# Subtracting k's maxima on VectorE out of PSUM, token tables as narrow as the tokens seen, and three rows for every free place: a fused linear attention, top-2 mixture of experts and soft mixture of experts on one Trainium2 core

## The chip, the cores and the metric

The program runs on one core of one Trainium2 chip. The metric is the device time of one execution in microseconds. A core has five engines that run their own instruction streams in order and wait for one another by semaphores: TensorE (PE in the rows, with its weight loads as PEld), VectorE (DVE), ScalarE (ACT), GpSimd (POOL) and SyncE (SP, which here only issues DMAs). Matmul results land in PSUM, everything else that the engines read and write is in SBUF, and DMAs move data between SBUF and DRAM.

## The reference, cut to what matters

```python
# attention, per batch and head (8 batches, 8 heads, 576 positions, 64 wide)
q_s = softmax(q, over the 64)          # q - max, exp, / sum
k_s = softmax(k, over the 576)         # k - np.max(k, axis=2), exp, / sum
kv = einsum('bhsd,bhse->bhde', k_s, v)
x = einsum('bhsd,bhde->bhse', q_s, kv) # -> x: 4608 tokens x 512

# mixture of experts: 8 experts, 512 -> 1024 -> 512, two per token
noisy = x @ w_gate + log1p(exp(x @ w_noise)) * noise
top2 = argpartition(-noisy, 2)[:, :2]; top2_w = softmax(noisy[top2])
for e in range(E):
    for k in range(2):
        mask = top2[:, k] == e
        out[mask] += top2_w[mask, k, None] * (relu(x[mask] @ w1[e]) @ w2[e])

# soft mixture of experts over out: logits = out @ phi (32 slots), softmax over
# tokens and over slots, 8 small experts on the slots, then c @ slot_out
```

The maximum of k runs over the positions, which lie on the partitions of a k tile, so it can't be taken by one reduction along the free axis.

## The kernel before

**Stages.** Attention takes the batches in four pairs (`i` = 0 to 3), each pair in nine tiles of 128 tokens: four whole tiles for the first batch, four for the second, and a ninth tile whose lower 64 partitions belong to the first batch and whose upper 64 to the second. A step list, `FIRST`, fixes the order in which the attention's steps are written: `lk`, `lv`, `lq` load, `km`/`ks`/`ke` take k's maxima, subtract them and apply exp for one batch of the pair, `qm`/`qs`/`qe` do the same for a third of the pair's q, `kv` multiplies k and v, `qt` transposes a q tile, `ou` makes the outputs of one tile, `ga` starts the gate of some tiles and `bg` advances it by a piece, `ze` writes zeros, `pf` and `pl` plan the experts. The framework's scheduler then places each engine's instructions by its own timeline, so the order on an engine follows the list only roughly. A second list, `MIX`, holds the last of the attention; it is interleaved with the first ten expert blocks.

**k's maxima** (`k_max`, `k_sub`, lines 200 to 226). For each batch of a pair, VectorE takes the maximum of the four whole tiles into `km` (L203, L205), then of `km` and the half tile (L207, 64 partitions). TensorE transposes `km` into a PSUM tile `pt` (L210), VectorE reduces it to `mT` (L212), TensorE transposes `mT` back, broadcast to all partitions, into another `pt` (L219), ScalarE copies that to SBUF as `ms` (L221), and GpSimd subtracts `ms` from the half tile (L223) and from the four whole tiles in two instructions of 1024 (L226). One of the eight cases, `ks0.1v`, has its three subtractions on VectorE. All `pt` tiles of this stage (also those of `qt`, `kt` and `kw`) come from one pool of three PSUM banks.

**Token tables.** Every pair's tokens go through a gate in two parts, of six tiles and of three (`gate`, lines 329 to 451). It ranks each token among those of its expert, writes the place as a row and a column, makes one-hot matrices of the rows (`ob`, L422, L423) and of the columns (`oa`, L431, 288 columns: 36 for each of 8 experts) on VectorE, multiplies them on TensorE (L441) and adds the result into the table `tab` (L446, or L449 to L451). The first half of the tokens (pairs 0 and 1) is planned first (`plan_first`), and its experts' blocks begin while the attention of pairs 2 and 3 runs.

**Expert blocks.** A block gathers rows of `xtab` by an index column for each 128 tokens (L694, GpSimd), transposes them (L766), multiplies by `w1` (L781) and `w2` (L811) and adds the weighted result to `x2` by a scatter that accumulates (L816 on VectorE, L817 on GpSimd). There are ten blocks of two index columns from the first half, then as many blocks of three columns as the plan asks for (five here, in nested branches, L902), then blocks of two. Gathers and scatters stand in one queue on GpSimd, in which gathers for a later block come ahead of a block's own scatters. Places of a table that no token fills get row `NTOK + p` of `xtab` and `x2`, one for each partition, so that two free places in one partition hit the same row. Scatters of one block of two are declared free of each other; the three scatters of a block of three are not, since free places occur there.

**Tail.** The soft mixture of experts reads `x2` back and ends the program.

Of the kernel before, what the change touches and what calls it, by code (L numbers as in the profile page):

```python
# [21 lines left out]
P = 128  # L22
# [12 lines left out]
TE = 36  # L35
NSLOT = 32
GT = 6
NZ, CW = 4, 6
EPS = 1e-9

# [31 lines left out]
def gate_consts(k, ap):  # L72
    nc = k.nc

    ltf = ap.tile([P, P], F32, name="ltf")
    nc.gpsimd.affine_select(out=ltf, in_=k.ones, pattern=[[1, P]], compare_op=ALU.is_gt, fill=0.0, base=0, channel_multiplier=-1)
    k.lt = ap.tile([P, P], F16, name="lt")
    nc.vector.tensor_copy(k.lt, ltf)
    k.ones16 = ap.tile([P, P], F16, name="ones16")
    nc.vector.tensor_copy(k.ones16, k.ones)  # L80

    it = ap.tile([P, E * TE], I32, name="it")
    nc.gpsimd.iota(it, pattern=[[1, E * TE]], base=0, channel_multiplier=0)
# [11 lines left out]
    k.eoff = ap.tile([P, E], F32, name="eoff")  # L95
    nc.vector.tensor_scalar(k.eoff, k.ef, float(TE * P), None, op0=ALU.mult)
    pd = ap.tile([P, 1], I32, name="pd")
    nc.gpsimd.iota(pd, pattern=[[0, 1]], base=NTOK + 1, channel_multiplier=1)
    k.pad1 = ap.tile([P, 1], F32, name="pad1")
    nc.vector.tensor_copy(k.pad1, pd)  # L100

    k.tril = ap.tile([P, E, E], F32, name="tril")
    nc.gpsimd.affine_select(out=k.tril, in_=k.ones[:, :64].rearrange("p (e f) -> p e f", e=E), pattern=[[1, E], [-1, E]], compare_op=ALU.is_gt, fill=0.0, base=0, channel_multiplier=0)

    k.tri = ap.tile([P, E + 1, E], F32, name="tri")
    nc.gpsimd.affine_select(out=k.tri, in_=k.ones[:, :72].rearrange("p (r e) -> p r e", e=E), pattern=[[1, E + 1], [-1, E]], compare_op=ALU.is_gt, fill=0.0, base=0, channel_multiplier=0)
    k.e7 = ap.tile([P, E], F32, name="e7")
    nc.vector.tensor_scalar(k.e7, k.ef, float(E) - 2.5, None, op0=ALU.subtract)


def attention(k):
# [3 lines left out]
    with ExitStack() as ctx:  # L115
# [27 lines left out]
        after = [None]  # L143
        cnt = ac.tile([P, E], F16, name="cnt")
        lgrs, rqas, seen = {}, {}, []
        tab = k.tab = ac.tile([P, E * TE], F32, name="tab")
        qts, kts, vts, qTs, kbTs = {}, {}, {}, {}, {}

# [20 lines left out]
        def zero(n):  # L169

            z = zz[n % 2]
            if n < 2:
                nc.gpsimd.memset(z, 0.0)

            nc.gpsimd.tensor_copy(z[:, 0:1], after[0][:, 0:1])
            nc.gpsimd.memset(z[:, 0:1], 0.0)
            if n == NZ:
                nc.sync.dma_start(k.xtab[NTOK:, :D], z)
                nc.sync.dma_start(k.xtab[NTOK:, D:], z[:, :E])
            half = k.x2[:NTOK // 2] if n < NZ else k.x2[NTOK // 2:]  # L180
            xr = half.rearrange("(p r) d -> p r d", p=P)
            n_r = half.shape[0] // P
            r = slice(n % NZ * n_r // NZ, (n % NZ + 1) * n_r // NZ)
            nc.sync.dma_start(xr[:, r], bcast(z, 1, r.stop - r.start))

        def setup():
            for i in range(2):
                for b in range(2):
                    nc.gpsimd.memset(KB[i][b], 0.0)
                    for h in range(2):  # L190
                        nc.gpsimd.memset(KB[i][b][h * 64:(h + 1) * 64, :, NW - 2 + h:NW - 1 + h], 1.0)
# [5 lines left out]
            nc.vector.memset(cnt, 0.0)  # L197


        def k_max(i, b):  # L200
            kt = kts[i]
            m2 = e2.tile([P, 2, D], F32, name="m2")
            nc.vector.tensor_max(m2, kt[:, 4 * b:4 * b + 2, :], kt[:, 4 * b + 2:4 * b + 4, :])  # L203
            km = e2.tile([P, D], F32, name="km")
            nc.vector.tensor_max(km, m2[:, 0, :], m2[:, 1, :])  # L205
            hr = slice(b * 64, b * 64 + 64)
            nc.vector.tensor_max(km[hr], km[hr], kt[hr, 8, :])  # L207
            pk = k.pt([P, 4, P])
            for c in range(4):
                nc.tensor.transpose(pk[:, c, :], km[:, c * P:(c + 1) * P], k.ident)  # L210
            mT = sp.tile([P, 4], F32, name="mT", bufs=2)
            nc.vector.tensor_reduce(mT, pk, axis=AX.X, op=ALU.max)  # L212
            return mT

        def k_sub(i, b, mT, engs):
            kt = kts[i]
            pk = k.pt([P, 4, P])
            for c in range(4):
                nc.tensor.transpose(pk[:, c, :], mT[:, c:c + 1].to_broadcast([P, P]), k.ident)  # L219
            ms = e2.tile([P, D], F32, name="ms", bufs=2)  # L220
            nc.scalar.copy(ms, pk.rearrange("p c d -> p (c d)"))  # L221
            hr = slice(b * 64, b * 64 + 64)
            engs[0].tensor_sub(kt[hr, 8, :], kt[hr, 8, :], ms[hr])  # L223
            for j2 in range(0, 4, 2):
                js = slice(4 * b + j2, 4 * b + j2 + 2)
                engs[j2 // 2].tensor_sub(kt[:, js, :], kt[:, js, :], bcast(ms, 1, 2))  # L226

        def k_exp(i, b):
            kt = kts[i]
# [98 lines left out]

        def gate(T0, T1):
            n_t = T1 - T0  # L330
            full = lambda n, s=None, d=F32: sp.tile(s or [P, GT, E], d, name=n)[:, :n_t]
            flat = lambda x: x.rearrange("p t e -> p (t e)")
            lr = lgrs[T0 // TP][:, T0 % TP:T0 % TP + n_t]
# [64 lines left out]
            nc.vector.tensor_tensor(pos, pk, bcast(k.eoff, 1, n_t), op=ALU.add)  # L398
# [28 lines left out]

            def columns(ms):
                n_p = ms.stop - ms.start
                oas.append(sp.tile([P, CW // 2, E * TE, 2], F16, name="oa", bufs=2)[:, :n_p])  # L430
# [6 lines left out]
            pa = pr.tile([P, E * TE], F32, name="pk")  # L437
            for ms in parts:
                oa = oas.pop(0)
                for m in range(2 * ms.start, 2 * ms.stop):  # L440
                    nc.tensor.matmul(pa, ob[:, m // 2, :, m % 2], oa[:, m // 2 - ms.start, :, m % 2], start=m == 0, stop=m == 2 * n_t - 1)  # L441
                if len(oas) and ms.stop < n_t - CW // 2:
                    columns(slice(ms.stop + CW // 2, ms.stop + CW))
                yield
            if T0 == 0:
                nc.vector.tensor_copy(tab, pa)  # L446
            else:
                tt = sp.tile([P, E * TE], F32, name="tt")
                nc.vector.tensor_scalar(tt, pa, 0.0, float(T0 * P), op0=ALU.is_gt, op1=ALU.mult)  # L449
                nc.vector.tensor_add(tab, tab, pa)  # L450
                nc.vector.tensor_add(tab, tab, tt)  # L451

        bg, fine = [], [False]

# [12 lines left out]
        def step(st):  # L467
# [10 lines left out]
            elif a == "km":  # L478
                mx["k", i, j] = k_max(i, j)
            elif a == "ks":  # L480
                k_sub(i, j, mx["k", i, j], engs)
            elif a == "ke":
                k_exp(i, j)
            elif a == "qm":
# [50 lines left out]
def table(k):  # L535
# [1 line left out]
    nc = k.nc  # L537
    m = k.ac.tile([P, E * TE + TE], F32, name="pl_m")
    nc.vector.memset(m[:, E * TE:], 0.0)
    nc.vector.tensor_scalar(m[:, :E * TE], k.tab, 0.0, k.pad1, op0=ALU.is_equal, op1=ALU.mult)  # L540
    nc.vector.scalar_tensor_tensor(m[:, :E * TE], k.tab, -1.0, m[:, :E * TE], op0=ALU.add, op1=ALU.add)
    return m

# [153 lines left out]
def experts(k, att, rs):  # L697

    nc, tc = k.nc, k.tc
    with ExitStack() as ctx:  # L700
# [55 lines left out]
            return t[:, c:c + 1]  # L756

        def gather(b, s):
            gather_rows(k, xg[s], at(b, s), NTOK // 2 if b < NPA else NTOK + P)

        def xpose(b, s):
            pt = bank("ph", [P, 4, P])
# [50 lines left out]
        def scatter(b, s, py):  # L813
# [479 lines left out]
def attention_moe_softmoe(ctx: ExitStack, tc: tile.TileContext, q, k, v, w_gate, w_noise, noise, w1, w2, phi, m1, m2, out):  # L1293
# [5 lines left out]
    s.xtab = dp.tile([NTOK + P, XC], F32, name="xtab")  # L1299
    s.x2 = dp.tile([NTOK + P, D], F32, name="x2")  # L1300
    s.ctx, s.n_regs = ctx, 0
    consts(s, ctx)
    att = attention(s)
# [53 lines left out]
```

## Time and profile before

| | |
|---|---|
| runs | 1258.68, 1257.89, 1254.75 us; median 1257.89 |
| profiled execution | 1253.2 us, of which the trace spans 1251.3 |
| busy, share of the span | PE 92%, PEld 80%, DVE 66%, ACT 47%, POOL 30% |
| granted TensorE clock, mean | 0.959 |

The shares are averages over stages with different limits. In the first seventh of the span VectorE is the busiest engine; from there to the tail TensorE is busy nearly all the time, with one gap. The rows that are quoted below give start and duration in microseconds of the profiled execution.

### The profile page before, as it was taken

To read this page: it belongs to the slowest core of one execution; us is meant where nothing else is said; L and a number is where in the kernel's file an instruction comes from. 1 tells how busy PE (TensorE), PEld (TensorE's weight loads), DVE (VectorE), ACT (ScalarE), POOL (GpSimd) and SP (SyncE) were. 2 spreads that over 40 slices of the span, in tenths; PEclk is the share of its full clock that TensorE was granted. 3 is DMA by queue.
4 is the path that set the end of the run, shared out by engine and by line. 5 is a ranking of instruction groups with operands and counts; after the bars stand their busy time and mean duration, and the time that the engine had idled before them with its cause. 6 is when DMAs were issued, how large, how long until landed. Compare 5 with 4: busy or idle time off the path is not lost. (4 is left out here: it accounts for less than half of the span.)

```text
span 1251.3 us, 21319 instructions
## 1 busy us (share of the span) xinstructions
PE 1151.5 (92%) x7792; PEld 1001.5 (80%) x7792; DVE 821.3 (66%) x1468; ACT 585.5 (47%) x887; POOL 371.0 (30%) x397
## 2 busy tenths in 40 slices
PE   4786789999999999999997999999999999978995
PEld 3675678998898898899986899899899899865542
DVE  7989978668786665455554666666666666654753
ACT  3555466464545444444443445444444444433324
POOL 6655653232352230222212242242231131120000
PEclk9877788999999999999998999999999999997997
DMA  9848244576356374566656656374645345137697
GB/s 342 293 153 286 102 145 154 160 247 201 78 152 152 95 219 143 160 169 170 166 161 204 187 134 204 74 226 106 203 101 171 68 101 136 34 57 302 226 379 305
DMA packets 115336, 218.01 MB, mean 174 GB/s; under 512 B 13712, under 2 KB 53776, under 8 KB 111120
## 3 DMA queue, kind: packets, MB, share of 16 engines
q1 hardware_dynamic: 98176, 176.05, 40.9%
q0 software_dynamic: 17040, 40.44, 17.1%
q8 instruction: 65, 1.06, 0.4%
q14 instruction: 55, 0.45, 0.1%
HBM read 243.31 MB, written 48.65 MB: 233 GB/s over the span
## 5 line engine op out<-in xcount | busy, mean ns | idle before, releaser
L748 DVE TENSOR_TENSOR R0l<-ringS,R0h 128x1024 fp32r<-128x1024 f32 x95 | 116.3, 1224 | 102.8 <-ACT R0h L748 96.0
L748 DVE TENSOR_TENSOR R1l<-ringS,R1h 128x1024 fp32r<-128x1024 f32 x96 | 117.5, 1224 | 100.6 <-ACT R1h L748 97.4
L748 DVE TENSOR_TENSOR R2l<-ringS,R2h 128x1024 fp32r<-128x1024 f32 x91 | 111.4, 1224 | 89.1 <-ACT R2h L748 81.3
L748 ACT ACTIVATE R1h<-ringS 128x1024 fp32r<-128x1024 f32 x96 | 101.7, 1060 | 139.2 <-PE py L811 84.1
L748 ACT ACTIVATE R0h<-ringS 128x1024 fp32r<-128x1024 f32 x95 | 100.8, 1061 | 137.0 <-PE py L811 75.9
L748 ACT ACTIVATE R2h<-ringS 128x1024 fp32r<-128x1024 f32 x91 | 96.5, 1060 | 144.1 <-PE py L811 81.3
L781 PE MATMUL ph<-xh,R0h 128*128 128x256 f32 x400 | 112.6, 282 | 1.1 <-DVEq L902 1.0
L694 POOL DMA_INDIRECT xg<-xtab,pl_idx x40 | 49.3, 1233 | 213.8 <-DVE sc L771 198.9
L781 PE MATMUL ph<-xl,R0h 128*128 128x256 f32 x400 | 112.6, 282 | 0.0
L781 PE MATMUL ph<-xh,R0l 128*128 128x256 f32 x400 | 112.2, 280 | 0.0
L785 DVE SCALAR_TENSOR_TENSOR hl<-ph,hh 128x512 fp32r<-128x512 f32 x140 | 95.7, 684 | 24.0 <-ACT hh L784 20.4
L781 PE MATMUL ph<-xh,R2h 128*128 128x256 f32 x360 | 102.2, 284 | 1.9 <-DVE hl L785 1.9
L781 PE MATMUL ph<-xl,R2h 128*128 128x256 f32 x360 | 102.0, 283 | 0.5 <-DVE xl L768 0.5
L781 PE MATMUL ph<-xh,R2l 128*128 128x256 f32 x360 | 101.8, 283 | 0.0
L817 POOL DMA_INDIRECT x<-y,pl_idx x40 | 63.5, 1588 | 128.9 <-DVE y L816 118.9
L781 PE MATMUL ph<-xh,R1h 128*128 128x256 f32 x360 | 100.8, 280 | 0.2 <-DVE hl L785 0.2
L781 PE MATMUL ph<-xl,R1h 128*128 128x256 f32 x360 | 100.4, 279 | 0.3 <-DVE xl L768 0.3
L781 PE MATMUL ph<-xh,R1l 128*128 128x256 f32 x360 | 100.3, 279 | 0.0
L784 ACT ACTIVATE hh<-ph 128x512 fp32r<-128x512 f32 x140 | 81.6, 583 | 32.5 <-PE ph L781 29.2
L811 PE MATMUL py<-R1l,hh 128*128 128x512 f32 x200 | 79.5, 398 | 0.0
L811 PE MATMUL py<-R1h,hl 128*128 128x512 f32 x200 | 78.8, 396 | 0.0
L781 PEld LDWEIGHTS ph<-xh,R0h 128*128 128x128 f32 x400 | 75.4, 189 | 2.3 <-issue 1.4
(440 smaller groups left out, 3133.7 us busy)
## 6 DMA issues: line engine op xcount, KB each, us to landing
ringS<-in_moe_w_dram SPq DMA_DIRECT2D x292, 512.0 KB
ringA<-in_moe_w_dram SPq DMA_DIRECT2D x12, 1024.0 KB
ringA<-in_moe_w_dram SPq DMA_DIRECT2D x22, 512.0 KB
xtab<-xr SPq DMA_DIRECT2D x36, 256.0 KB
kt<-in_k_dram SPq DMA_DIRECT2D x8, 1024.0 KB
v<-in_v_dram SPq DMA_DIRECT2D x8, 1024.0 KB
x<-z SPq DMA_DIRECT2D x5, 1280.0 KB
ringS<-x SPq DMA_DIRECT2D x5, 1024.0 KB
```

The lines of the kernel that those rows point to most:

```text
L694: k.nc.gpsimd.indirect_dma_start(out=x, out_offset=None, in_=k.xtab[:n], in_offset=bass.IndirectOffsetOnAxis(ap=idx, axis=0))
L748: turn[1:] = [nc.scalar.activation(r[0], f, AF.Copy), nc.vector.tensor_sub(r[1], f, r[0].bitcast(F32))]
L781: nc.tensor.matmul(ph[:, g, :], w[i][:, c, g * P:(g + 1) * P], x[:, c, :], start=n == 0, stop=n == 11)
L784: nc.scalar.activation(hh[:, fs, :], ph, AF.Relu)
L785: nc.vector.scalar_tensor_tensor(hl[:, fs, :], ph, 0.0, hh[:, fs, :].bitcast(F32), op0=ALU.max, op1=ALU.subtract)
L811: nc.tensor.matmul(py[s], a[h], w[i][:, f, :], start=u == 4 and f == n == 0, stop=u == 7 and f == 1 and n == 2)
L817: d = nc.gpsimd.indirect_dma_start(out=k.x2[:NTOK // 2] if b < NPA else k.x2, out_offset=bass.IndirectOffsetOnAxis(ap=at(b, s), axis=0), i ...
```

## The change

Three things are edited.

- **k's maxima.** `k_max` no longer takes the half tile into `km`. Once for each pair it transposes the ninth tile into a `pt` bank, reduces each half of it (one instruction for both batches) to `m8`, and takes the maximum of `mT` and `m8`, 128 x 4. `k_sub` leaves out ScalarE's copy: VectorE subtracts the PSUM tile itself from k, in all eight cases.
- **Token tables.** A gate that ends at tile `T1` uses `8 * T1` columns where 288 stood: in `oa`, in the matmuls, and in what is added to `tab`, which is set to zero at the start. (At the eight gates `T1` is 6, 9, 15, 18, 24, 27, 33, 36.)
- **Free places.** The rows beyond the tokens are 384 in place of 128, and a free place takes one of three by its column, so that three columns side by side never share a row. The three scatters of a block of three are declared free of each other as well. The zeros written there grow likewise.

```diff
+NFREE = 3
 ...
-            hr = slice(b * 64, b * 64 + 64)
-            nc.vector.tensor_max(km[hr], km[hr], kt[hr, 8, :])
+            if i not in m8s:
+                m8s[i] = sp.tile([P, 4, 2], F32, name="m8", bufs=2)
+                pk = k.pt([P, 4, P])
+                for c in range(4):
+                    nc.tensor.transpose(pk[:, c, :], kt[:, 8, c * P:(c + 1) * P], k.ident)
+                nc.vector.tensor_reduce(m8s[i], pk.rearrange("p c (b s) -> p c b s", b=2), axis=AX.X, op=ALU.max)
 ...
             nc.vector.tensor_reduce(mT, pk, axis=AX.X, op=ALU.max)
+            nc.vector.tensor_max(mT, mT, m8s[i][:, :, b])
 ...
-            ms = e2.tile([P, D], F32, name="ms", bufs=2)
-            nc.scalar.copy(ms, pk.rearrange("p c d -> p (c d)"))
+            ms = pk.rearrange("p c d -> p (c d)")
-            engs[0].tensor_sub(kt[hr, 8, :], kt[hr, 8, :], ms[hr])
...
-                engs[j2 // 2].tensor_sub(kt[:, js, :], kt[:, js, :], bcast(ms, 1, 2))
+                nc.vector.tensor_sub(kt[:, js, :], kt[:, js, :], bcast(ms, 1, 2))
+            nc.vector.tensor_sub(kt[hr, 8, :], kt[hr, 8, :], ms[hr])
 ...
-                nc.vector.tensor_tensor(oas[-1], bcast(k.cols, 1, n_p), over(af, ms, E * TE), op=ALU.is_equal)
+                nc.vector.tensor_tensor(oas[-1], bcast(cols, 1, n_p), over(af, ms, n_c), op=ALU.is_equal)
 ...
-            for o in puts.get(b, []) if b < THREE else []:
+            for o in puts.get(b, []):
                 tc.declare_no_dep(d.ins, o.ins, reason="other rows")
```

**What stands on GpSimd**, around the subtractions of the second pair (`kt` is k, `q` and `qt` are q, `v` is v's column of ones, `lgr` the gate's logits). Before:

```order
L156 MEMSET v_748 128x36
L223 TENSOR_TENSOR kt<-kt,ms 64x512
L226 TENSOR_TENSOR kt<-kt,ms 128x1024 x2
L246 TENSOR_TENSOR qt<-qt,qm 128x1536 x3
L223 TENSOR_TENSOR kt<-kt,ms 64x512
L226 TENSOR_TENSOR kt<-kt,ms 128x1024 x2
L316 TENSOR_TENSOR lgr<-lgr,rqa 128x128
```

And with the change:

```order
L255 TENSOR_TENSOR q_164<-q_164,qm 128x1536
L158 MEMSET v_758 128x36
L255 TENSOR_TENSOR qt<-qt,qm 128x1536 x3
L325 TENSOR_TENSOR lgr<-lgr,rqa 128x128
L336 TENSOR_TENSOR lgr<-lgr 128x3x64
```

The six k instructions are gone from GpSimd; q's subtractions and the gate's sums follow each other.

**What stands on VectorE** at the same place (`qm` is q's maximum, `pt` a PSUM bank, `m_...` the maxima of two tiles and with the change also `m8`). Before:

```order
L212 TENSOR_REDUCE mT<-pt 128x4
L277 TENSOR_TENSOR KB_130<-pv,rk 64x4x64 x2
L205 TENSOR_TENSOR km<-m_358 128x512
L239 TENSOR_REDUCE qm<-qt 128x24
L207 TENSOR_TENSOR km<-km,kt 64x512
L239 TENSOR_REDUCE qm<-qt 128x24 x2
L306 TENSOR_SCALAR rqa<-pv 128x8
L212 TENSOR_REDUCE mT<-pt 128x4
```

And with the change:

```order
L221 TENSOR_REDUCE mT<-pt 128x4
L209 TENSOR_TENSOR km<-m_365 128x512
L248 TENSOR_REDUCE qm<-qt 128x24
L222 TENSOR_TENSOR mT<-mT,m_247 128x4
L248 TENSOR_REDUCE qm<-qt 128x24
L234 TENSOR_TENSOR kt<-kt,pt 128x1024 x2
L235 TENSOR_TENSOR kt<-kt,pt 64x512
L248 TENSOR_REDUCE qm<-qt 128x24
L221 TENSOR_REDUCE mT<-pt 128x4
```

The maximum with the half tile (L207) is gone, and the three subtractions (L234, L235) stand between two of q's reductions, with the 128 x 4 maximum ahead of them.

**What GpSimd waits for in a block of three** (L694 and L709 are the gathers, L817 and L832 the scatters; in brackets the semaphores waited for, `DMASW` those of GpSimd's own DMAs, numbered in turn from 0 to 7). Before:

```order
L694 DMA xg_1812<-xtab,pl_id_4338 128x520 [waits DMASW3_49,DMASW1_49,PE_49]
L694 DMA xg_1815<-xtab,pl_id_4338 128x520 [waits DMASW4_49,PE_49]
L694 DMA xg_4438<-xtab,pl_id_4338 128x520 [waits DMASW5_49,PE_49]
L817 DMA x_58<-y,pl_id_4338 4736x512 [waits DMASW0_49,DVE_49]
L817 DMA x_58<-y,pl_id_4338 4736x512 [waits DMASW4_49,DVE_49]
L817 DMA x_58<-y,pl_id_4338 4736x512 [waits DMASW5_49,DVE_49]
```

And with the change:

```order
L709 DMA xg_1823<-xtab,pl_id_4349 128x520 [waits DMASW3_49,DMASW1_49,PE_49]
L709 DMA xg_1826<-xtab,pl_id_4349 128x520 [waits DMASW4_49,PE_49]
L709 DMA xg_4449<-xtab,pl_id_4349 128x520 [waits DMASW5_49,PE_49]
L832 DMA x_58<-y,pl_id_4349 4992x512 [waits DMASW0_49,DVE_49]
L832 DMA x_58<-y,pl_id_4349 4992x512 [waits DVE_49]
L832 DMA x_58<-y,pl_id_4349 4992x512 [waits DMASW6_49,DVE_49]
```

The three scatters carry semaphores 4, 5 and 6. Before, the second waits for the first and the third for the second; now the second waits for VectorE alone, and the third for number 6, its own, which the DMA eight places earlier in the queue used, a scatter of the block before.

## Rows read from the trace of the kernel before

**Rows 1.** Busy time by stage: from:to, length, engines, TensorE clock, DMA share, GB/s.

```profile
0.00:60.00 60.00, 37.13 (x212) 31.75 (x212) 50.17 (x64) 25.09 (x32) 39.86 (x45) 0.91 0.97 331
60.00:181.00 121.00, 89.32 (x571) 78.04 (x571) 109.19 (x262) 69.54 (x156) 68.69 (x84) 0.80 0.48 165
181.00:470.00 289.00, 284.33 (x1898) 255.95 (x1895) 207.50 (x438) 149.99 (x229) 97.35 (x130) 0.99 0.58 164
656.00:670.00 14.00, 5.31 (x22) 4.30 (x21) 1.23 (x1) 1.64 (x2) 2.00 (x2) 0.76 0.48 130
```

**Rows 2.** Timeline of VectorE: start, us, what, in brackets idle time before.

```profile
40.07 7.44 DVE L207 TENSOR_TENSOR km<-km,kt 64x512 f32<-64x512 f32 x1
...
52.91 0.68 DVE L318 TENSOR_TENSOR xr<-pv,rqa 128x512 f32<-128x512 f32 x1
...
92.73 6.68 DVE L422 TENSOR_TENSOR ob<-cols,bf 128x768 f16<-128x768 f16 x2
...
146.60 5.12 DVE L376 TENSOR_TENSOR r<-r,r 128x24 f32<-128x24 f32 x1
```

**Rows 3.** Timeline of GpSimd at three of these places.

```profile
39.59 4.65 POOL L226 TENSOR_TENSOR kt<-kt,ms 128x1024 f32<-128x1024 f32 x2
...
49.37 5.48 POOL L246 TENSOR_TENSOR qt<-qt,qm 128x1536 f32<-128x1536 f32 x2 [2.42 <-DVE qm L239]
...
147.05 4.63 POOL L226 TENSOR_TENSOR kt<-kt,ms 128x1024 f32<-128x1024 f32 x2
```

**Rows 4.** Waits of TensorE from 20 to 181 us: total, times, longest.

```profile
PE pk L441 <- DVE ob L423: 8.4, 2, 7.9
PE pt L210 <- DVE km L207: 7.4, 2, 6.3
PE pt L283 <- DVE KB L277: 6.7, 2, 6.5
```

**Rows 5.** VectorE's groups by shape, 0 to 220 us: busy, mean ns, idle before.

```profile
L207 DVE TENSOR_TENSOR km<-km,kt 64x512 f32<-64x512 f32 x8 | 12.6, 1578 | 0.2
...
L431 DVE TENSOR_TENSOR oa<-cols,af 128x1728 f16<-128x1728 f16 x9 | 9.2, 1045 | 0.0
...
L212 DVE TENSOR_REDUCE mT<-pt 128x4 f32<-128x512 f32 x8 | 5.4, 680 | 1.2 <-PE pt L210 1.2
...
L226 DVE TENSOR_TENSOR kt<-kt,ms 128x1024 f32<-128x1024 f32 x2 | 2.4, 1222 | 0.0
...
L449 DVE TENSOR_SCALAR tt<-pk 128x288 f32<-128x288 f32 x4 | 1.8, 449 | 2.9 <-PE pk L441 2.9
```

**Rows 6.** GpSimd's subtractions from k, the same view, same stretch.

```profile
L226 POOL TENSOR_TENSOR kt<-kt,ms 128x1024 f32<-128x1024 f32 x14 | 34.2, 2462 | 0.2
...
L223 POOL TENSOR_TENSOR kt<-kt,ms 64x512 f32<-64x512 f32 x7 | 9.7, 1388 | 15.7 <-ACT ms L221 15.6
```

**Rows 7.** Chain of waits around 650 us: start, us, what.

```profile
639.63 4.87 DMA x<-y,pl_id
...
645.27 7.07 DMA x<-y,pl_id
...
653.08 6.75 DMA x<-y,pl_id
...
661.41 3.39 DMA xg<-xtab,pl_idx
...
665.80 3.40 PE py L811 x10
```

**Rows 8.** TensorE's timeline behind that chain, and the chain one block later, undisturbed.

```profile
664.93 0.87 PE L766 MATMUL ph<-ident,xg 128*128 128x128 f32 x3 [8.69 <-DMA xg<-xtab,pl_idx]
...
690.31 2.30 PE py L811 x10
```

**Rows 9.** The last two scatters (timeline of GpSimd) and what follows their landing (chain).

```profile
1118.74 1.61 POOL L817 DMA_INDIRECT x<-y,pl_idx  x1 [16.55 <-DVE y L816]
...
1127.25 0.02 SPq L973
```

More of the change, by code (lines that the diff above doesn't have):

```diff
@@ L94, in gate_consts @@
     nc.vector.tensor_copy(k.tok1, tk.unsqueeze(2).to_broadcast([P, GT, 2]))
[L95 to L99, printed above, removed]
+    pd = ap.tile([P, NFREE], I32, name="pd")
+    nc.gpsimd.iota(pd, pattern=[[P, NFREE]], base=NTOK + 1, channel_multiplier=1)
+    k.pad1 = ap.tile([P, NFREE], F32, name="pad1")
     nc.vector.tensor_copy(k.pad1, pd)
@@ L145, in attention @@
         lgrs, rqas, seen = {}, {}, []
+        m8s = {}
         tab = k.tab = ac.tile([P, E * TE], F32, name="tab")
@@ L177, in zero @@
             if n == NZ:
-                nc.sync.dma_start(k.xtab[NTOK:, :D], z)
-                nc.sync.dma_start(k.xtab[NTOK:, D:], z[:, :E])
+                free = k.xtab[NTOK:].rearrange("(s p) c -> p s c", p=P)
+                nc.sync.dma_start(free[:, :, :D], bcast(z, 1, NFREE))
+                nc.sync.dma_start(free[:, :, D:], bcast(z[:, :E], 1, NFREE))
             half = k.x2[:NTOK // 2] if n < NZ else k.x2[NTOK // 2:]
@@ L197, in setup @@
             nc.vector.memset(cnt, 0.0)
+            nc.vector.memset(tab, 0.0)
         def k_max(i, b):
@@ L212, in k_max, with k_sub @@
             nc.vector.tensor_reduce(mT, pk, axis=AX.X, op=ALU.max)
+            nc.vector.tensor_max(mT, mT, m8s[i][:, :, b])
             return mT
-        def k_sub(i, b, mT, engs):
+        def k_sub(i, b, mT):
             kt = kts[i]
@@ L330, in gate @@
             n_t = T1 - T0
+            n_c = E * T1
+            cols = k.cols[:, :n_c]
+            tabs = tab.rearrange("p (e c) -> p e c", e=E)[:, :, :T1]
             full = lambda n, s=None, d=F32: sp.tile(s or [P, GT, E], d, name=n)[:, :n_t]
@@ L397, in gate @@
             pos = full("pos")
-            nc.vector.tensor_tensor(pos, pk, bcast(k.eoff, 1, n_t), op=ALU.add)
+            nc.vector.scalar_tensor_tensor(pos, bcast(k.ef, 1, n_t), float(T1 * P), pk, op0=ALU.mult, op1=ALU.add)
             nc.vector.tensor_mul(pos, pos, s16)
@@ L429, in columns @@
                 n_p = ms.stop - ms.start
-                oas.append(sp.tile([P, CW // 2, E * TE, 2], F16, name="oa", bufs=2)[:, :n_p])
-                nc.vector.tensor_tensor(oas[-1], bcast(k.cols, 1, n_p), over(af, ms, E * TE), op=ALU.is_equal)
+                oas.append(sp.tile([P, CW // 2, E * TE, 2], F16, name="oa", bufs=2)[:, :n_p, :n_c])
+                nc.vector.tensor_tensor(oas[-1], bcast(cols, 1, n_p), over(af, ms, n_c), op=ALU.is_equal)
             for ms in parts[:2]:
@@ L436, in gate @@
             yield
-            pa = pr.tile([P, E * TE], F32, name="pk")
+            pa = pr.tile([P, E, T1], F32, name="pk")
             for ms in parts:
@@ L440, in gate @@
                 for m in range(2 * ms.start, 2 * ms.stop):
-                    nc.tensor.matmul(pa, ob[:, m // 2, :, m % 2], oa[:, m // 2 - ms.start, :, m % 2], start=m == 0, stop=m == 2 * n_t - 1)
+                    nc.tensor.matmul(pa.rearrange("p e c -> p (e c)"), ob[:, m // 2, :, m % 2], oa[:, m // 2 - ms.start, :, m % 2], start=m == 0, stop=m == 2 * n_t - 1)
                 if len(oas) and ms.stop < n_t - CW // 2:
@@ L445, in gate @@
             if T0 == 0:
-                nc.vector.tensor_copy(tab, pa)
+                nc.vector.tensor_copy(tabs, pa)
             else:
-                tt = sp.tile([P, E * TE], F32, name="tt")
+                tt = sp.tile([P, E * TE], F32, name="tt")[:, :n_c].rearrange("p (e c) -> p e c", e=E)
                 nc.vector.tensor_scalar(tt, pa, 0.0, float(T0 * P), op0=ALU.is_gt, op1=ALU.mult)
-                nc.vector.tensor_add(tab, tab, pa)
-                nc.vector.tensor_add(tab, tab, tt)
+                nc.vector.tensor_add(tabs, tabs, pa)
+                nc.vector.tensor_add(tabs, tabs, tt)
         bg, fine = [], [False]
@@ L480, in step @@
             elif a == "ks":
-                k_sub(i, j, mx["k", i, j], engs)
+                k_sub(i, j, mx["k", i, j])
             elif a == "ke":
@@ L539, in table @@
     nc.vector.memset(m[:, E * TE:], 0.0)
-    nc.vector.tensor_scalar(m[:, :E * TE], k.tab, 0.0, k.pad1, op0=ALU.is_equal, op1=ALU.mult)
+    by3 = lambda x: x.rearrange("p (t c) -> p t c", c=NFREE)
+    nc.vector.scalar_tensor_tensor(by3(m[:, :E * TE]), by3(k.tab), 0.0, bcast(k.pad1, 1, E * TE // NFREE), op0=ALU.is_equal, op1=ALU.mult)
     nc.vector.scalar_tensor_tensor(m[:, :E * TE], k.tab, -1.0, m[:, :E * TE], op0=ALU.add, op1=ALU.add)
@@ L758, in gather @@
         def gather(b, s):
-            gather_rows(k, xg[s], at(b, s), NTOK // 2 if b < NPA else NTOK + P)
+            gather_rows(k, xg[s], at(b, s), NTOK // 2 if b < NPA else NTOK + NFREE * P)
         def xpose(b, s):
@@ L1298, in attention_moe_softmoe @@
     dp = ctx.enter_context(tc.tile_pool(name="dram", bufs=1, space=DRAM))
-    s.xtab = dp.tile([NTOK + P, XC], F32, name="xtab")
-    s.x2 = dp.tile([NTOK + P, D], F32, name="x2")
+    s.xtab = dp.tile([NTOK + NFREE * P, XC], F32, name="xtab")
+    s.x2 = dp.tile([NTOK + NFREE * P, D], F32, name="x2")
     s.ctx, s.n_regs = ctx, 0
```

## The prediction

> **What bounds the kernel now.** I read the stage table first, to see which engine fills which stretch [rows 1]. From 0 to 181 us VectorE is busy for 50.17 + 109.19 = 159.4 us (88%), TensorE for 37.13 + 89.32 = 126.5 at a clock of 0.91 and 0.80, so VectorE sets the end of the attention. DMA is at 0.97 in the first 60 us: k, v and q of the first pairs are still arriving, and a shorter VectorE gains little there. From 181 us TensorE is busy (284.33 of 289), and what another engine saves is worth nothing, except where TensorE stands: from 656 to 670 us it works 5.31 of 14 us.
>
> Next, how long single instructions of VectorE take [rows 2] and what GpSimd does meanwhile [rows 3]. A 64x512 maximum lasts 7.44 us from 40.07, while GpSimd subtracts from 39.59 to 44.24; a 128x24 operation lasts 5.12 us from 146.60, GpSimd's subtraction runs from 147.05 to 151.68, and the two end 0.04 us apart. But a 128x512 multiplication that reads PSUM takes 0.68 us at 52.91, in the middle of a subtraction of GpSimd (49.37 to 54.85). So an instruction of VectorE with both inputs in SBUF is held while GpSimd subtracts, and part of the 159.4 us is no work. The third view, TensorE's waits, shows who pays: its three largest are for VectorE's `ob`, `km` and `KB`, 22.5 us in all, and the longest single ones (7.9, 6.3, 6.5) fall on those holds [rows 4].
>
> Last, the chain of waits around 650 us. The three scatters of the last block of three follow one another, issued at 639.63, 645.27 and 653.08, each after the landing of the one before; the last lands at 659.83, the branch ends, a gather runs from 661.41 to 664.80 [rows 7], and TensorE has waited for it for 8.69 us [rows 8].
>
> **Term 1: k's maxima and the tables, all on VectorE from 0 to 181 us.**
>
> *Added.* Seven of the eight cases move from GpSimd: 14 subtractions of 1024 at 1.222 us (VectorE's own two in the eighth case [rows 5]) and seven of 512 at 0.68 (the 512-wide multiplication [rows 2]), 17.1 + 4.8 = 21.9. Four reductions to `m8` at 0.68, as to `mT`, 2.7. Eight maxima of 128x4: 288 columns take 0.449 and 512 take 0.680 [rows 5], so a column costs 1.03 ns and an instruction 0.15 us beside its columns; 8 x 0.16 = 1.3. Together 25.9.
>
> *Removed.* Eight L207, at 0.68 without the hold: 5.4. The columns of `oa`: nine instructions take 9.2 us [rows 5], of which 9 x 0.15 is fixed; the first six gates keep 8 x T1 of 288 columns, 0.44 of the rest, so 7.8 x 0.56 = 4.4; I take 4 (3 to 5). The three table operations of five gates: 0.30 of 0.449 us is columns, and 12/36 to 27/36 go, 2.4 in sum over the gates, so 3 x 0.30 x 2.4 = 2.2; with the new zeroing 2 (1 to 2.4). And the holds under GpSimd's seven subtractions from k, 43.9 us of GpSimd's time, 6.3 for each case [rows 6]. In the three cases of [rows 2], VectorE loses 4.2 us (40.07 to GpSimd's end at 44.24), 5.6 (6.68 less two instructions of 768 columns at the 0.52 ns a column of `oa`, 1.1 in all) and 4.95 (5.12 less its own 0.17), 14.8 in sum: that is the lower bound. If all seven hold alike, 7 x 4.9 = 34. I take 27, 3 for each case not shown: a third of the time VectorE reads PSUM or reduces there, which isn't held. Removed 5.4 + 4 + 2 + 27 = 38.4, net 12.5 us less VectorE. At the bounds: 25.9 - 24.2 = 1.7 us more, or 46.8 - 25.9 = 21 less. VectorE sets the end for 88% of the stage, so 0.88 x 12.5 = **11 us** (from 1.5 lost to 18).
>
> What hides the rest. ScalarE loses eight copies; it isn't the bound (69.5 of 121 us, [rows 1]). TensorE gets 16 more transposes; three such take 0.87 us [rows 8], so 16 x 0.29 = 4.6, in a stage where it stands still for 54 us, and narrower table matmuls give part of it back. Without that cover it would cost 4.6. The further zeros (256 rows of 4128 bytes, 1.06 MB) are written while TensorE is busy for 284.33 of 289 us and DMA at 0.58: I charge nothing; at the 331 GB/s of the loads it is 3.2 us, if weights were late by as much.
>
> GpSimd's subtractions from q stay, and hold VectorE as before [rows 3]; they can even move against other victims. That is in the bounds.
>
> [...] The row at 52.91 (PSUM input, 512 wide) takes 0.68 us and the SBUF-fed fixed part above gives 0.15 + 512 x 1.03 ns, also 0.68, so I charge nothing. [...] By the rows, 11.
>
> **Term 2: the free places, at the end of the blocks of three.** The scatters no longer wait for each other's landing. Issue takes GpSimd 1.61 us; of the last pair the first is issued at 1118.74, the second behind it, and both have landed at 1127.25, 8.5 us after the first [rows 9]. With 0.3 us between issues, three from 639.63 stand 1.9 us apart, and the third is issued at 643.4; the longest landing in [rows 7] is 7.07, so the third lands at 650.5 instead of 659.83. The 1.58 us to the gather and its 3.39 stay: it lands at 655.5, where TensorE is ready at 664.93 - 8.69 = 656.24. So the whole idle time goes, and with it the slow clock behind it, 3.40 instead of 2.30 for ten matmuls: 9.8 at most. If each transfer takes 10 us beside the others, the gather lands at 658.4, 2.2 us late. I take **9 us** (3 to 9.8). In the earlier blocks of three the same serial scatters hold nobody (284.33 of 289, and no wait of TensorE for them), so only the last one pays. Late next is VectorE's work or the gather itself, within a microsecond of TensorE.
>
> **Sum.** 1253.2 (profiled execution) - 11 - 9 = 1233.2. The median of the runs, 1257.9, lies 4.7 above that execution; the forecast is 1257.9 - 20 = **1238**.
>
> **The rivals.**
>
> *A: the attention gives nothing.* The holds end, but VectorE carries 25.9 us of its own more, or the loads (DMA 0.97 in the first 60 us) set the pace of the first pairs. For: the lower bound of the holds. Against: the three holds of [rows 2], on which TensorE's longest waits fall, start at 40, 93 and 147 us, two of them behind the loads. Term 1 zero: 1257.9 - 9 = 1249.
>
> *B: the three scatters take turns in the DMA engines.* Their durations add as now, 4.87 + 7.07 + 6.75 = 18.7, and only the two pauses of 0.75 go: gain 1.5, 1257.9 - 11 - 1.5 = 1245. For: DMA is busy with weights there. Against: the two scatters of [rows 9] land within 8.5 us, less than any two of [rows 7] in turn. [...]
>
> *C, slower: k's subtraction holds a PSUM bank.* Before, ScalarE emptied the bank at once; now it is free only after VectorE's third subtraction, 2 x 1.222 + 0.68 = 3.1 us at best, later if VectorE has other work first. Three banks serve all transposes of the stage, and TensorE, in order, stops when the next is taken; it waits 14.1 us for such banks' users already [rows 4]. If each of the eight cases stops it for the full 3.1, it is 24.8 us, which makes 1238 + 25 = 1263. It decides from 20 / 8 = 2.5 us per case. Against: TensorE can go two banks ahead, and those waits are two single stops of 6.3 and 6.5 us, on held instructions.
>
> *D: the change doesn't do what it says.* The order on GpSimd shows that k's subtractions and the waits between the scatters are gone, so only its worth is open.
>
> **How the numbers follow.** Forecast 1238, 0.60, its own range 1230 to 1247 by the bounds of the two terms; A 1249, 0.17; B 1245, 0.11; both 1256, 0.05; C 1263, 0.07. The range 1226 to 1251 holds the forecast with its bounds, A and B, and leaves out both and C, and some of the tails. About 0.3%, 3.8 us, is what a measurement can tell from no change: the border is 1254. Faster: forecast, A, B and a little of both, 0.88; within: 0.05; slower: C, 0.07.
>
> **What would show it.** In the profile of the changed kernel: no k subtraction on GpSimd; 24 on VectorE near 1.2 and 0.68 us; VectorE's long 128x24 and 64x512 instructions left only under q's subtractions; its busy time in the attention about 13 us less, and TensorE continuously busy some 11 us before 181. At the end of the threes three scatters about 1.9 us apart and a wait for the gather below 2 us. Wrong would be: VectorE's busy time as before (A), scatters that land 6 us apart (B), new waits of TensorE for `pt` on VectorE's subtraction (C).

## The result, and the profile after

| | before | changed |
|---|---|---|
| median | 1256.32 us (1254.24 to 1258.68) | 1233.78 us (1230.92 to 1239.40) |
| profiled execution: span | 1251.3 | 1232.9 |
| granted TensorE clock, mean | 0.959 | 0.967 |

The ratio is 0.9841, 95% interval 0.9812 to 0.9870: 20 us faster, as forecast (1238). Run once more beside the experiments, the changed kernel had 0.9848 (0.9817 to 0.9880).

Where the 18.4 us between the two profiled executions lie is read from three instants. The first expert matmul from `R1h` starts at 193.83 instead of 206.53: 12.7 us. The first scatter of the last block of three is issued at 625.13 instead of 639.63: 14.5. Ten matmuls behind the gap end at 648.21 instead of 669.20: 21.0. The last pair's first scatter stands at 1097.76 instead of 1118.74: still 21.0; and the tail is 2.6 us longer. So this pair of traces puts 14.5 us in the attention and what follows up to the scatter, and 6.5 in the gap, with 2.6 given back in a tail that the change doesn't touch (133 to 136 us long in the other runs). One trace is one execution: in a second one of the changed kernel the first expert matmul starts at 197.67 and that first scatter is issued at 628.92, 3.8 us later in both. Differences of that size between two traces say nothing.

The stage table of the changed kernel, which answers to [rows 1] (from:to, length, engines, TensorE clock, DMA share, GB/s):

```profile
0.00:60.00 60.00, 40.63 (x205) 34.47 (x206) 48.02 (x73) 26.04 (x31) 22.21 (x36) 0.89 0.94 322
60.00:181.00 121.00, 96.49 (x679) 83.36 (x678) 101.25 (x308) 71.57 (x166) 49.11 (x93) 0.89 0.58 201
```

VectorE (third of the engines) does more instructions in less time, GpSimd (fifth) is down from 39.86 and 68.69 us, and TensorE's granted clock from 60 to 181 us is 0.89 on average instead of 0.80. How much of the gain that clock gives back wasn't separated. Up to the first expert matmul VectorE is busy for 161.5 us; in the kernel before it was 178.9:

```profile
0.00:193.80 193.80, 146.89 (x954) 126.50 (x954) 161.49 (x421) 104.44 (x209) 77.34 (x138) 0.89 0.69 237
```

```profile
0.00:206.50 206.50, 150.21 (x934) 129.95 (x934) 178.90 (x391) 108.63 (x216) 121.11 (x158) 0.84 0.65 222
```

VectorE's groups of the changed kernel, 0 to 210 us (busy, mean ns, idle before), which answer to [rows 5]:

```profile
L234 DVE TENSOR_TENSOR kt<-kt,pt 128x1024 f32<-128x1024 f32 x16 | 18.8, 1212 | 2.5 <-PE pt L229 2.4
...
L222 DVE TENSOR_TENSOR mT<-mT,m 128x4 f32<-128x4 f32 x8 | 2.4, 302 | 0.1
```

The subtractions of 1024 cost what was forecast, and so do those of 512 and the reductions to `m8`, with 0.68 us each. The 128x4 maximum, forecast at 0.16 us, takes 0.30 on average (0.15 in the run below that has q's subtractions off GpSimd too). The three largest waits of TensorE (20 to 181 us) sum to 13.6 us, where [rows 4] has 22.5:

```profile
PE pt L229 <- DVE mT L222: 5.9, 2, 4.0
PE pv L312 <- DVE lgr L328: 4.3, 1, 4.3
PE pk L395 <- DVE tab L460: 3.4, 1, 3.4
```

No wait of TensorE up to 200 us is for a bank that k's subtraction holds (rival C). The chain around the end of the threes (start, us, what), which answers to [rows 7] and [rows 8]:

```profile
628.93 11.07 DMA x<-y,pl_id
...
641.27 3.98 DMA xg<-xtab,pl_idx
...
645.90 2.30 PE py L826 x10
```

The three scatters are issued at 625.13, 627.05 and 628.93, 1.9 us apart as forecast; the third takes 11.07 us, and TensorE waits 0.59 us for the gather. But a wait that the forecast didn't have stands ahead of it, right behind the branch (timeline of TensorE: start, us, in brackets idle time before it; the stage row behind it has the granted clock, 0.51, as third number from the end):

```profile
628.36 0.39 PE L796 MATMUL ph<-xh,R0h 128*128 128x256 f32 x1 [2.39 <-ACT R2h L763]
...
645.38 0.52 PE L781 MATMUL ph<-ident,xg 128*128 128x128 f32 x3 [0.59 <-DMA xg<-xtab,pl_idx]
```

```profile
628.60:632.00 3.40, 3.40 (x18) 3.40 (x18) 0.71 (x1) 0.00 (x0) 1.82 (x2) 0.51 0.97 273
```

In the kernel before, TensorE stood 0.99 us there. From 628.6 to 632.0 us of the changed kernel TensorE runs at a granted clock of 0.51, and its matmuls take 0.41 us in place of 0.28; from 632 the clock is 0.99 again. The kernel before kept 1.00 behind its stop. The longer stop (1.4 us) and the slower matmuls (some 1.6) make TensorE ready for the gather 3.1 us later, counted from the first scatter, than before (19.7 us instead of 16.6).

### The profile page after: what moved, and what is told of

It reads as the page before. It is cut to its first block, busy times and chain, and to the rows that moved or that the text cites. A ratio compares the mean times of both kernels' runs of the same rounds, so it can differ in the third digit from the quotient of the medians.

```text
span 1232.9 us, 21326 instructions
## 1 busy us (share of the span) xinstructions
PE 1148.2 (93%) x7808; PEld 997.7 (81%) x7808; DVE 802.4 (65%) x1493; ACT 580.7 (47%) x879; POOL 326.9 (27%) x376
## 5 line engine op out<-in xcount | busy, mean ns | idle before, releaser
L709 POOL DMA_INDIRECT xg<-xtab,pl_idx x40 | 49.2, 1229 | 216.7 <-DVE sc L786 198.1
L832 POOL DMA_INDIRECT x<-y,pl_idx x40 | 63.5, 1588 | 129.0 <-DVE y L831 118.9
```

Source lines behind the costliest of these rows:

```text
L709: k.nc.gpsimd.indirect_dma_start(out=x, out_offset=None, in_=k.xtab[:n], in_offset=bass.IndirectOffsetOnAxis(ap=idx, axis=0))
```

## The experiments

Two theories were to be told apart. **Holding:** GpSimd's subtractions lengthen VectorE's instructions with two SBUF inputs, and what pays is that they are gone. **Chain:** what pays is a shorter chain from k's maxima to exp. Beside them stood the shares of the parts and the forecast's zeros. The ratios are to the kernel before of the same chip and runs; the us are the ratio's difference from 1, times 1254.

| run | ratio, 95% interval | us | first expert matmul | VectorE busy up to it |
|---|---|---|---|---|
| kernel before | | | 206.5 | 178.9 |
| changed (first comparison) | 0.9841 (0.9812 to 0.9870) | -20.0 | 193.8 | 161.5 |
| k's part alone | 0.9941 (0.9921 to 0.9961) | -7.4 | 197.6 | 162.6 |
| free places alone | 0.9943 (0.9921 to 0.9964) | -7.1 | 214.1 | 177.1 |
| narrow tables alone | 1.0006 (0.9985 to 1.0026) | +0.8 | 203.4 | 177.7 |
| changed, scatters in turn | 0.9921 (0.9897 to 0.9946) | -9.9 | 194.7 | 165.7 |
| changed, again | 0.9848 (0.9817 to 0.9880) | -19.1 | 197.7 | 162.7 |
| changed, ScalarE's copy | 0.9877 (0.9852 to 0.9902) | -15.4 | 195.7 | 163.0 |
| changed, k on GpSimd | 0.9934 (0.9912 to 0.9956) | -8.3 | 203.4 | 163.7 |
| changed, load on GpSimd | 1.0026 (1.0007 to 1.0045) | +3.3 | 215.1 | 180.9 |
| subtractions alone | 0.9910 (0.9883 to 0.9937) | -11.3 | 194.8 | 164.7 |
| ninth tile's maxima alone | 1.0130 (1.0099 to 1.0161) | +16.3 | 221.3 | 181.3 |
| changed, q on VectorE | 0.9960 (0.9940 to 0.9981) | -5.0 | 207.9 | 172.3 |
| before, 16 more transposes | 1.0106 (1.0080 to 1.0133) | +13.3 | 217.5 | 182.3 |

The last two columns (us) are of one execution each.

**The parts.** k's part alone takes the edits of `k_max` and `k_sub` as the diff has them.

> k's part alone: the ninth tile's maxima by TensorE and VectorE, k's subtractions on VectorE out of PSUM; tables and free places as before. Theory (VectorE is no longer held by GpSimd's subtractions): 6 to 9 us below the kernel before, the first expert matmul at 198 to 200 us instead of 206.5, VectorE busy 8 to 10 us less until the experts start, the wait of 8.7 us for the gather at the end of the blocks of three still there. Rival A (VectorE only swaps holding for work of its own): within 3 us of the kernel before. Rival C (k's subtraction holds a PSUM bank): slower by up to 25 us, with waits of TensorE for a bank of about 3 us in each case.

Measured -7.4 us, the first expert matmul at 197.6: as the theory had it; rivals A and C are out. The wait for the gather is there (7.6 us). But VectorE's busy time falls by 16.3 us (178.9 to 162.6), twice the 8 to 10 expected, for 7.4 us of time: less than half of it passes.

The free places alone:

> The free places alone: 384 rows, the three scatters of a block of three declared free of each other. Theory: the three are issued 1.9 us apart, the wait for the gather falls from 8.7 to below 1 us, and the time by 6 to 9 us, to about 1249. Rival B (the scatters take turns in the DMA engines): 1.5 us. In the trace of the changed kernel TensorE stood 2.4 us behind the last branch and ran 8 us at the lower clock after it; if that comes with the three scatters it is here too, if it comes with the attention's shift it is not, and the gain is 3 us larger.

Measured -7.1 us. Its profiled execution (1256.64 us) is the longest of its seven, median 1247.44, and its first expert matmul is late (214.1), so of its trace only the gap is read: a wait of 3.7 us for the gather, 0.99 us behind the branch.

```profile
PE ph L771 <- DMA xg<-xtab,pl_idx: 3.7, 1, 3.7
PE ph L786 <- DVEq L907: 1.0, 1, 1.0
```

So the forecast of a wait below 1 us was wrong; the chain shows the gather landing 20.2 us after the first scatter is issued, in the changed kernel 20.1 (625.13 to 645.25), and TensorE is ready after 16.6 us unless something else delays it. In the changed kernel the longer stop behind the branch and the lower clock (0.51; 3.4 us at it, not 8) fill that difference: its short wait of 0.59 us is there because TensorE came late. The stop and the lower clock don't come with the scatters: the 95 matmuls behind the 0.99 us take 11.41 us here, 0.12 each, where at 0.51 they start 0.21 apart. From the first scatter of the last block of three to that of the last pair this trace has 475.06 us, 4.1 less than the kernel before (479.11); where the rest of the 7.1 lies it doesn't show.

The tables alone:

> The narrow token tables alone, all else as before. Theory (VectorE sets the pace of the attention, whatever it works on): 6 us less VectorE, 4 to 6 us less time. Rival (the table steps lie in stretches where VectorE waits or in the gates' own chain): less than 2 us.

Measured +0.8, its interval from 1.9 us faster to 3.3 slower: the theory's 4 to 6 us are out. VectorE is busy for 177.66 us up to 203.4, 1.2 less than before, though the columns are gone: other instructions became longer. One `w` of 128x24, for instance, now falls under two of GpSimd's subtractions from k, which run from 96.89 to 101.54 us:

```profile
96.77 4.81 DVE L344 TENSOR_SCALAR w<-u 128x24 f32<-128x24 f32 x1
```

It has one SBUF input, so instructions with two are not the only ones held. The kernel before shows the same: a cast of 128x6 (L408) takes 2.74 us from 131.55, in a subtraction of q's on GpSimd from 131.51 to 134.27. Since VectorE's total hardly fell, this run doesn't say whether that total sets the end; the run with k on GpSimd, below, does.

The changed kernel without the declaration, `for o in puts.get(b, []) if b < THREE else []:`

> The changed kernel, but the three scatters of a block of three again wait for each other; the 384 rows and the larger zeros stay. Theory: the wait for the gather of about 8.7 us comes back and the time is 6 to 8 us above the changed kernel, 1240 to 1242; the rows and zeros cost nothing. Rival (the gain came from elsewhere, the scatters were hidden): within 2 us of the changed kernel.

Measured -9.9 us against the kernel before, where the changed kernel run again has -19.1: the free scatters are worth 9 us here (two comparisons, with intervals of 3 to 4 us to each side), the wait is back (6.3 us, and the ten matmuls take 4.02), the rows and zeros cost nothing that shows.

**The changed kernel again** is the anchor for the next three:

> The changed kernel once more, unedited, so that the next three have it beside them on the same chip: 1232 to 1236 us, 18 to 22 below the kernel before. By the parts run alone the sum is 7.4 + 7.1 + 0 = 14.5; if this gives 14 to 16, the first comparison flattered the change, if it gives 18 to 22 the parts help each other.

-19.1, where the parts alone give 7.4 + 7.1 - 0.8 = 13.7. The four intervals together leave an estimated 6 us of doubt (half widths of 2.5, 2.7, 2.6 and 4.0 us, added as squares), so the 5.4 us between them aren't clear of noise. That the parts help each other is not shown, though the runs below show that an edit in this kernel can move more than its own work.

**Is it PSUM?** The copy put back:

```diff
-            ms = pk.rearrange("p c d -> p (c d)")
+            ms = e2.tile([P, D], F32, name="ms", bufs=2)
+            nc.scalar.copy(ms, pk.rearrange("p c d -> p (c d)"))
```

> The changed kernel, but ScalarE copies the PSUM bank to SBUF again and VectorE subtracts from there. It asks two things of the PSUM operand. Theory (what counts is that GpSimd no longer subtracts): within 3 us of the changed kernel. Rival C (the bank held by the subtraction costs TensorE): faster than the changed kernel by 3 us or more. Rival (the shorter chain of k pays): 8 copies of 0.59 us and their hand-over on the path, 4 to 6 us slower.

3.7 us slower than the changed kernel, with intervals that overlap from 0.9852 to 0.9880: not clear of noise, and it doesn't decide between the two other readings. Rival C (faster by 3 us or more) is out. What the operand does is seen on the instruction itself (all 16, duration in ns: shortest, median, longest). From PSUM, in the changed kernel:

```profile
L234 DVE TENSOR_TENSOR kt<-kt,pt x16: 1201/1212/1222, 12.5 to 151.2; 128x1024 f32<-128x1024 f32 x16
```

From SBUF, with the copy:

```profile
L235 DVE TENSOR_TENSOR kt<-kt,ms x16: 1209/1218/3781, 13.1 to 156.0; 128x1024 f32<-128x1024 f32 x16
```

The undisturbed duration is the same; under q's subtractions, which stay on GpSimd, the one with two SBUF inputs goes up to 3.78 us, the one that reads PSUM never over 1.22. The same two subtractions of the second pair show it, in the changed kernel (GpSimd subtracts from q from 42.22 to 47.70) and with the copy (42.84 to 52.02):

```profile
43.79 2.34 DVE L234 TENSOR_TENSOR kt<-kt,pt 128x1024 f32<-128x1024 f32 x2
```

```profile
47.02 6.08 DVE L235 TENSOR_TENSOR kt<-kt,ms 128x1024 f32<-128x1024 f32 x2
```

The sixteen take 25.1 us in place of 18.8. At the median the form that reads PSUM takes 1.212 us and the one from SBUF 1.218, so a charge for the PSUM source isn't seen.

**Is it GpSimd?** The copy, and the subtractions back on GpSimd in seven cases of eight:

```diff
-                nc.vector.tensor_sub(kt[:, js, :], kt[:, js, :], bcast(ms, 1, 2))
+                engs[j2 // 2].tensor_sub(kt[:, js, :], kt[:, js, :], bcast(ms, 1, 2))
 ...
```

> The changed kernel, but k's subtractions go back to GpSimd, from ScalarE's copy, seven cases of eight as in the kernel before; the ninth tile's maxima stay as changed. VectorE has 22 us less of its own work, but is held again. Theory: 5 to 9 us above the changed kernel, and VectorE's operations with two SBUF inputs are long again under L226-like subtractions. Rival (dropping the maximum with the half tile is what pays, the engine doesn't matter): within 2 us.

10.8 us slower than the changed kernel, 7.1 than the one with the copy. Up to the first expert matmul VectorE is busy for 163.66 us here (first row) and 162.98 with the copy (second):

```profile
0.00:203.40 203.40, 153.88 (x946) 136.29 (x946) 163.66 (x400) 106.94 (x215) 119.00 (x160) 0.85 0.66 225
```

```profile
0.00:195.70 195.70, 145.35 (x947) 124.88 (x947) 162.98 (x421) 107.67 (x216) 75.25 (x139) 0.87 0.68 234
```

That is 22 us less work of its own, and as much more holding. So in this pair the holding and the own work are equal in size, VectorE's total is the same, and yet the end comes 7.1 us later: VectorE's total alone doesn't set it. What is left is the shorter way from k's maxima to exp, 3.1 us in place of 6.3 for each case, and q's subtractions, which no longer queue behind k's; these two weren't separated. The same move in the kernel before (the subtractions alone, below) does lower VectorE's total, by 14.2 us, so the equality belongs to this pair. The rival is out.

The load on a scratch tile, beside the changed kernel's own work:

```diff
 ...
+            if (i, b) != (0, 1):
+                nc.gpsimd.tensor_copy(scr[:, 2, 0:4], mT)
+                nc.gpsimd.tensor_sub(scr[hr, 0, :], scr[hr, 0, :], scr[hr, 2, :])
+                for j2 in range(2):
+                    nc.gpsimd.tensor_sub(scr[:, 0:2], scr[:, 0:2], bcast(scr[:, 2], 1, 2))
```

> The changed kernel with a load added: in seven of the eight cases GpSimd also does the three subtractions that it did before, of the same sizes, on a scratch tile that nobody reads, started by the same maxima. VectorE's work and k's chain are as in the changed kernel, so only the holding (and GpSimd's time, for q's subtractions behind it) comes back. Theory (holding): VectorE's busy time until the experts start rises by 15 to 30 us, and the time by 10 to 20. Rival (the long instructions were coincidence, or what paid was k's chain): VectorE's busy time rises by less than 5 us and the time by less than 4.

22.4 us slower than the changed kernel, all of the gain. VectorE does the same 421 instructions up to the first expert matmul as in the changed kernel, and is busy for 180.93 us in place of 161.49:

```profile
0.00:215.10 215.10, 152.89 (x946) 132.11 (x946) 180.93 (x421) 104.05 (x208) 120.90 (x168) 0.84 0.62 213
```

19.4 us of holding for 42.8 us of GpSimd's instructions (33.9 + 8.9). q's subtractions stand behind the load on GpSimd, so the 22.4 us needn't all be holding; but the chain theory alone (less than 4 us) falls.

**The two halves of k's part.** The subtractions alone, `L207` kept:

> The kernel before with one half of k's part: the subtractions on VectorE straight from PSUM; the maximum with the half tile stays as it was. Theory (the subtractions leaving GpSimd is what pays, by freeing VectorE from holds and by shortening k's chain): 5 to 8 us below the kernel before, nearly all of what k's part gave (7.4). Rival (the maxima pay): less than 2 us.

-11.3 us: beyond the theory's 5 to 8, at least as much as the whole of k's part (-7.4; the intervals overlap) and as the whole attention part of the changed kernel (-9.9). VectorE is busy for 164.7 us up to the first expert matmul, 14.2 less than before, although some 22 us of work were added, so an estimated 36 us of holding went (14.2 + 22). `L207`, which is the same code and took 12.6 us there [rows 5], shows it:

```profile
L207 DVE TENSOR_TENSOR km<-km,kt 64x512 f32<-64x512 f32 x8 | 5.4, 679 | 0.2
```

The ninth tile's maxima alone, the subtractions on GpSimd:

> The other half of k's part: the ninth tile's maxima once for each pair by TensorE and one reduction from PSUM; the subtractions stay on GpSimd. The changed kernel with the subtractions on GpSimd had VectorE busy for 164 us until the experts start, 15 less than the kernel before, yet gained at most 2 us in time with this and the tables. Theory: 0 to 2 us below the kernel before. Rival (VectorE's busy time sets the end whatever it is spent on): 8 us or more.

16.3 us slower: both theories missed. VectorE's small maximum is among the victims now (group of eight, total and mean):

```profile
L219 DVE TENSOR_TENSOR mT<-mT,m 128x4 f32<-128x4 f32 x8 | 16.7, 2082 | 0.1
```

A 128x4 instruction with both inputs in SBUF takes 2.08 us on average (0.15 to 7.32) in the kernel where GpSimd subtracts k; the same takes 0.30 in the changed kernel, and 1.23 with the load. It stands in k's chain, and TensorE waits 7.6 us for it once. Two waits are longer, though, both for the gate's work: 7.7 us for `ob` and 11.0 for `ai`. How the 16.3 us split among them isn't separated:

```profile
PE pv L306 <- DVE ai L417: 11.0, 1, 11.0
...
PE pt L226 <- DVE mT L219: 7.6, 1, 7.6
```

**The zeros of the forecast.** Sixteen more transposes in the kernel before:

```diff
-            for c in range(4):
+            for c in [0, 1, 2, 3, 0, 1, 2, 3] if b == 0 else range(4):
                 nc.tensor.transpose(pk[:, c, :], km[:, c * P:(c + 1) * P], k.ident)
```

> The kernel before with sixteen more transposes on TensorE in the attention, the first of each pair's maxima done twice over, which changes nothing but TensorE's work and the count of its instructions (16 more, as with the changed kernel). They cost at most 4.6 us of a TensorE that waits there. Every kernel with the ninth tile's transposes showed TensorE standing for 2.1 to 3.2 us behind the last branch of the threes, those without it 1.0. Theory 1 (the place of TensorE's code decides that wait): 2 to 3 us there, and the lower clock behind it. Theory 2 (something else of k's part): 1.0 as in the kernel before. The time: within 3 us of the kernel before.

13.3 us slower, where at most 4.6 us of TensorE's work were added to an engine that stood still for 54 us. In the stretch from 60 to 181 us VectorE does 219 instructions in place of 262:

```profile
60.00:181.00 121.00, 85.95 (x537) 76.41 (x536) 103.60 (x219) 62.67 (x124) 65.96 (x77) 0.80 0.42 145
```

The order on every engine is another from the second pair on (on GpSimd, sums of the gate have moved ahead of q's subtractions), and what GpSimd holds is other work: two `oa` take 7.71 us from 98.53, one `pos` 5.61 from 161.19, both while GpSimd subtracts from k (98.72 to 105.32, 160.87 to 166.73).

How much is the transposes and how much the order that the scheduler laid anew isn't separated by this run. The wait behind the last branch is 2.6 us here, as in the kernels with the ninth tile's transposes, although k's part is the old one. The kernel with q on VectorE, which has those transposes too, stops twice there, 0.99 us at the branch (up to 642.66) and 0.84 three matmuls on (up to 644.10).

So every kernel with sixteen more transposes lost 1.8 to 3.2 us there, and the four without them (before, free places, tables, subtractions alone) 1.0. This speaks against theory 2: the wait comes with sixteen more transposes, also without k's changed part (2.6 us). That it is the place of TensorE's code, as theory 1 has it, was the author's reading; no run here shows it.

**More of the same?** q's subtractions on VectorE as well: `q_sub(i, j, mx["q", i, j], (nc.vector, nc.vector))`

> The changed kernel with q's subtractions on VectorE too, 11 of 1536 elements that stand on GpSimd now, some 1.75 us each, 19 us of VectorE's own work. The added load of 42.8 us on GpSimd lengthened VectorE's busy time by 19.4 us, 0.45 of its own time; by that share q's 31.3 us cost VectorE 14 us by holding. Theory (a step should move when the holds that it ends exceed its own time on VectorE): net 5 us more VectorE, 2 to 6 us slower than the changed kernel. Rival (any GpSimd subtraction is better moved): 3 us or more faster.

14 us slower than the changed kernel: the sign of the theory, but not its size. q's subtractions cost VectorE 12 x 1.75 us, with both inputs in SBUF, and its busy time up to the first expert matmul is 172.27 us, 10.8 more; that matmul came 10 to 14 us later (207.9 against 197.7 and 193.8 in the two executions of the changed kernel).

The runs point to a version that was not run: the changed kernel with `L207` in place of the ninth tile's transposes. The subtractions alone gave 3.9 us more than with them, which isn't clear of noise.

## Why the prediction held, and where it didn't

The time and both terms came out, and two of the edits that were to pay did: k's subtractions leaving GpSimd, and the scatters set free. The tables didn't. That the sum of term 1 came out is luck, since its items missed to both sides.

- **What bounds the kernel** held in part: VectorE up to the experts, some of it holding. With the load on GpSimd the same VectorE work takes 19.4 us longer and the end comes 22.4 us later, though GpSimd's own queue grew as well. But VectorE's total isn't all: with k on GpSimd it is within 1 us of the run with the copy, and the end 7.1 us later.
- **Term 1, forecast 11 us, measured 9.9** (changed kernel with scatters in turn; 12.7 and 8.9 at the first expert matmul of the two traces). The holding taken away was put at 27 us between 15 and 34. The load gives 19.4, the copy against k on GpSimd about 22, the subtractions alone about 36: it depends on what the scheduler puts under GpSimd's subtractions. The tables were put at 6 of 12.5 us, and give nothing that shows by themselves. The subtractions alone gave 11.3 where the forecast's items for them leave 5 (27 - 21.9); their chain, 3.1 in place of 6.3 us in each case, was named for no gain. (Of the columns of the tables 9/36 to 27/36 go, not 12/36; the sum of 2.4 is right.)
- **The weakest step** is the cover: "TensorE gets 16 more transposes ... in a stage where it stands still". That an engine stands still over a stage doesn't mean that its next instruction is free. In the kernel before, these sixteen came with 13.3 us, the new order included, three times the 4.6 that were named as the price without cover; transposes and order weren't separated. Inside k's part the ninth tile's maxima cost 3.9 us (not clear of noise) instead of saving 1.4 of VectorE.
- **0.88 as the share that passes** isn't borne out as one number: 14.2 us less VectorE gave 11.3 (subtractions alone), 16.3 gave 7.4 (k's part), 19.4 more cost 22.4 (load).
- **Term 2, forecast 9 us, measured 7.1 alone and 9 as the last part**; the two traces put 6.5 in the gap. The issue 1.9 us apart was right. The transfers were mis-sized: 7.07 taken for the third, 11.07 measured (10.0 to 10.7 in four other runs), just above the bound of 10. Three scatters land in 14.9 us (625.13 to 640.00) instead of 20.2 (639.63 to 659.83), so rival B was right in part. A pair of scatters alone is no measure for three: the DMA share is 0.55 at 72 GB/s while the pair of [rows 9] runs (1118.74 to 1127.25), and 0.95 at 249 GB/s while the third of three does in the changed kernel (629 to 640), beside the loads of weights.
- **Rivals.** A fell for the whole, but is what the tables did. C fell: no wait of TensorE in the changed kernel is for its banks (one of 0.4 us with k's part alone), and ScalarE's copy, which takes 0.59 us where the three subtractions hold the bank for 3.1 (2 x 1.212 + 0.68), didn't make the kernel faster. Slower versions there were (16 transposes, load, q), none with the waits of C.
- **No charge for PSUM** held: 1.212 us from PSUM, 1.218 from SBUF (the rows behind the prediction's fixed part, L212 and L449 of [rows 5], both read PSUM, so they compared nothing), and the difference that matters was on the other side, since the subtraction with a PSUM operand wasn't held.

## What to carry to other kernels

Look at how long small instructions of VectorE take while GpSimd works: a 128x4 maximum of 2.08 us on average, with 0.15 as its shortest, is not work. Whether moving GpSimd's step to VectorE pays isn't told by VectorE being faster at it (1.21 us against 2.46 for 1024 of k, 1.75 against 2.76 for 1536 of q): k paid 11 us, q, with both inputs in SBUF, cost 14. A PSUM operand kept k's subtractions from being held (never over 1.22 us, against 3.78), but most of the gain was there from an SBUF copy as well; k's shorter chain may be what tells the two apart, which wasn't tested. And where a scheduler lays the order anew after each edit, a free addition to a waiting engine is a guess: 16 transposes came with 13 us.

## What was not expected of the hardware

- The third of three scatters in flight takes 10.0 to 11.1 us, where scatters in turn take 4.7 to 7.7 each, yet three together save 5.3 of 20.2 us.
- TensorE stood 1.0 us behind the last branch in the four traces without the 16 transposes and 1.8 to 3.2 us in the ten with them. In the changed kernel the longer stop (2.39 us) is followed by 3.4 us at a granted clock of 0.51, with matmuls of 0.41 us in place of 0.28; the kernel before, after 0.99 us, kept 1.00.
